# A half pair's value matmuls in one slot, the 64x64 group first: a thresholded attention with a routed MLP

## The chip, the cores and the metric

The kernel runs on one core of a Trainium2 chip. The metric is the device time of one execution in microseconds. The kernel before took 994.81 us (median of three runs, 994.56 to 995.75).

A core has engines that each work through a queue of their own in order: TensorE (PE; its weight loads are listed as PEld), VectorE (DVE), ScalarE (ACT), GpSimd (POOL) and SyncE (SP, which issues most of the transfers). They wait for each other by semaphores. TensorE writes to PSUM, from where VectorE and ScalarE read; everything else lies in SBUF.

## The reference, cut to what matters

```
q, k, v: (8 batches, 8 heads, 576 positions, 64), tau = 0.02
scores = q @ k^T / sqrt(64)
thresh = max(scores, last axis) - tau
scores = where(scores >= thresh, scores, -1e9)
attn   = exp(scores - max);  attn = attn / (sum(attn) + 1e-9)
x      = (attn @ v), as 4608 rows of 512

logits = x @ w_gate                                   # 8 experts, 576 rows each
take the (row, expert) pairs by falling logit, skip rows that have an expert
and experts that are full
out[rows of e] = relu(x[rows of e] @ w1[e]) @ w2[e]   # 512 -> 1024 -> 512
```

The change lies in the first part, the attention, and there in the product attn @ v.

## The kernel before, in words

**Pairs, tiles, slots.** The 64 heads are worked on as 32 pairs p (batch b = p // 4, j = p % 4). A pair has nine score tiles of 128 rows and 576 columns: tile i < 8 holds 128 queries of head i % 2, and tile 8, the short tile, holds the last 64 queries of both heads. The 288 tiles run through a pipeline of slots with two tiles each. In slot s the tiles 2s+4 and 2s+5 get their scores, 2s+2 and 2s+3 are masked, 2s and 2s+1 are transposed. Nine slots are two pairs, so a slot's place is told by its number modulo 9, its *class*; slots 0 to 8 are classes 0 to 8. The short tile of an even pair is scored in class 2 (first of the two tiles), that of an odd pair in class 6 (second).

**What a tile goes through.** `score` (L60) makes the scores with TensorE, in a PSUM tile `sc` of two banks; there are two such tiles. An ordinary tile is two matmuls on 64 rows and 128 columns of the array (64*128 in the profile), a short tile four on 64x64. `mx` (L71) scales them on VectorE into `z` and takes the row minimum of the negated scores (L74), which frees `sc`; GpSimd adds tau (L75). `ex` takes the exponential on ScalarE (L86). A slot later `stt` masks the result on VectorE and sums it (L90). Then `tr` transposes the tile with TensorE (L98, 64*128 as well) into the one PSUM tile `tb`, and in the next slot `trev` copies it on ScalarE into `pt` (L113, L115). Columns 512 to 575 of all tiles are transposed apart: `left` (L117) puts them into unused columns of the second `sc` tile of the slot, and `leftev` (L122) copies them on ScalarE into `pl` (L125 to L128). This is done in classes 4 and 8 (first part) and 5 and 0 (second part).

**Values.** attn @ v of a pair is made in two halves f of the queries: columns 0 to 255 (f=0) and 256 to 575 (f=1), each in a PSUM bank of its own, both named `xo`. A half has four units (`pv_unit`, L140): each two matmuls with all 128 rows and 64 columns of the array (128*64, L146). Keys that don't fit into these blocks are added by `pl_unit` (L147): two matmuls for each half, four in all on four 64x64 tiles of the array (L154), called the group here. Half 0 needs tiles 0 to 3 of a pair transposed, half 1 and the group need all nine. When a half is complete ScalarE copies it to `xt` (L155).

**Gates.** When the fourth pair of a batch is done, `finish` queues four pieces for the router's logits (`lg_unit` for either half, `lgt_unit`, `lgm_unit`), and in batches 0 and 1 five pieces that turn x back to rows and copy it out (`xt_unit`, L215 on VectorE). Each has TensorE work and, a slot later, ScalarE or VectorE work; they take the second `xo` bank in turn with half 1.

**What sets the order.** Every engine's instructions are in the order in which the Python code issues them. A slot issues: the scores, the left transposes, the copies left over from the slot before (`flush`, L255), `trev`, `mx`, `ex`, `leftev`, `stt`, loads for pair p+2 behind the short tile's scores, then `columns` (L259) and `whole` (L273), and last `tr`. `columns` takes units from the head of a queue that `push_pair` (L226) fills, in the order half 0, half 1, group. It spreads them: the number for a slot is what is left of the pair at the head, divided by the slots up to `last_slot` (L258). That makes one or two units, or one or two units and the group, in every slot. `whole` issues at most one gate a slot, when the second bank is free.

After the last scores (slot 141) the rest is issued without limit: the last two pairs' values, the logits of the last batch, and the preparation of the router for the first seven batches (`R.prep` and `R.compare`, L372 on VectorE). The routed MLP behind it (L787, L819 and others) isn't touched.

Of the kernel before, what the change touches and what calls it, by code (L numbers as in the profile page):

```python
# [13 lines left out]
AF = mybir.ActivationFunctionType  # L14
# [8 lines left out]
def attention(ctx, tc, qk, vl, tau, wgd, xrows, xts, Lg, nb_batches, ident, swap, R, after_first):  # L23
    nc=tc.nc
    V=nc.vector; A=nc.scalar; G=nc.gpsimd; T=nc.tensor
    NP=nb_batches*4; NT=NP*9
# [10 lines left out]
    LD={}  # L37
# [22 lines left out]
    def score(t):  # L60

        p,i=divmod(t,9); kd=LD[p]
        sc=ps_s.tile([128,2,512],F32,name="sc"); SC[t]=sc
        if i<8: todo=((i%2,slice(0,128),slice(i//2*128,i//2*128+128)),)
        else: todo=((0,slice(0,64),slice(512,576)),(1,slice(64,128),slice(512,576)))
        for h,o,c in todo:
            for f in range(2):
                r=slice(64*f,64*f+64)
                T.matmul(sc[o,f,:HS], kd["q",h][r,c], kd["k",h][r,:],start=True,stop=True)  # L69
# [25 lines left out]
    PT={}; PL={}; TB={}  # L95
# [36 lines left out]
    have={}  # L132
    XT={}; XO={}

    banks=([[True]],[[True]])
    def bank_v(sh,n):
        banks[n].append([False])
        return ps_v.tile(sh,F32,name="xo%d"%n)
    def free_v(n): return banks[n][-1][0]
    def pv_unit(p,f,u):  # L140
        b,j=divmod(p,4)
        if b not in XT: XT[b]=wk.tile([128,4,S],F32,name="xt",bufs=XTB)
        if u==0: XO[p,f]=bank_v([128,512],f)
        xo=XO[p,f]; q=FQ[f]; v=LD[p]["v"]
        for h in range(2):
            T.matmul(xo[64*h:64*h+64,:q.stop-q.start],v[:,f,128*u+64*h:128*u+64*h+64],PT[p][:,h,u,q],start=(u==0),stop=False,skip_group_check=True)  # L146
    def pl_unit(p,fs=(0,1)):  # L147

        b,j=divmod(p,4); r=[]
        for f in fs:  # L150
            xo=XO.pop((p,f)); q=FQ[f]; n=q.stop-q.start
            for a in range(2):
                g=slice(64*a,64*a+64); h=a^f
                T.matmul(xo[64*h:64*h+64,:n],LD[p]["v"][g,f,512:576],PL[p][g,q],start=False,stop=True,skip_group_check=True)  # L154
            r.append((banks[f][-1],lambda xo=xo,q=q,n=n: A.activation(XT[b][:,j,q],xo[:,:n],AF.Copy)))  # L155
        have[p,"pv"]=1
        return r
    def bank_g(b,sh):
        if b<nb_batches-1: return bank_v(sh,1)
        t=ps_s.tile([128,2,512],F32,name="sc")[:,0]  # L160
        return t.rearrange("p (a b) -> p a b",a=sh[1]) if len(sh)==3 else t

    RD={}
    def rd_calc(b):
        rd=wk.tile([128,4,9],F32,name="rd",bufs=XTB+NBO); RD[b]=rd
        V.tensor_scalar(rd,DEN[b],1e-9,None,op0=ALU.add)
        V.reciprocal(rd,rd)
    LT={}
    def lg_unit(b,f):
        if f==0: LT[b]=wk.tile([128,S+D],F32,name="lt",bufs=LTB)  # L170
        ps=bank_g(b,[128,512]); q=FQ[f]; n=q.stop-q.start; rd=RD[b]
        for j in range(4):
            T.matmul(ps[32*j:32*j+32,:n],wg[:,j],XT[b][:,j,q],start=True,stop=True,tile_position=(0,32*j))  # L173
# [51 lines left out]
    queue=[]; aux=[]; later=[]; late=[]; late2=[]; st={"last":-9,"slot":0}  # L225
    def push_pair(p):  # L226
        b,j=divmod(p,4)
        def when(n): return lambda: have.get((p,n),1<<30)+HOLD<=st["slot"]
        if p==NP-1:


            def left(f):
                for k,g in pl_unit(p,(f,)): g(); k[0]=True
            for f in range(2):
                for u in range(4): queue.append(("c",when("t3" if f==0 else "t8"),0 if u else f+1,lambda f=f,u=u: pv_unit(p,f,u),p))
                if f==0: queue.append(("n",when("t8"),False,lambda: rd_calc(b),p))
            for g in (lambda: left(0),lambda: left(1),lambda: lg_unit(b,0)(),lambda: lg_unit(b,1)(),lambda: lgt_unit(b)(),lambda: lgm_unit(b)()):
                queue.append(("n",when("pl"),False,g,p))
            queue.append(("n",lambda: not later,False,lambda: late.extend([lambda k,c=c: xt_unit(b,c,k) for c in range(5)]),p))
            return  # L240
        for f in range(2):
            for u in range(4): queue.append(("c",when("t3" if f==0 else "t8"),0 if u else f+1,lambda f=f,u=u: pv_unit(p,f,u),p))
            if (f,j)==(0,3): queue.append(("n",when("t8"),False,lambda: rd_calc(b),p))
        queue.append(("c",when("pl"),False,lambda: pl_unit(p),p))
        if (b,j)==(0,0): queue.append(("n",lambda: True,False,R.consts,p))
        if (b,j)==(nb_batches-1,2): queue.append(("n",lambda: not aux,False,lambda: (R.prep(0,28),R.compare(R.k("E1"),J,0,28)),p))
        if j==3: queue.append(("n",lambda: not later,False,lambda: finish(b),p))
    def finish(b):
        aux.extend([(0,lambda: lg_unit(b,0)),(0,lambda: lg_unit(b,1)),(1,lambda: lgt_unit(b)),(0,lambda: lgm_unit(b))])
        rows=[lambda k=1,c=c: xt_unit(b,c,k) for c in range(5)]  # L250
        if nb_batches-NDEF-NBO<=b<nb_batches-NDEF:
            nc.sync.dma_start(xts[b],XT[b]); late2.extend(rows)
        elif b<nb_batches-NDEF: aux.extend([(0,x) for x in rows])
        else: late.extend(rows)
# [32 lines left out]
    for s_ in range(-2,NT//2+2):  # L287
        st["slot"]=s_
        sc_=[t for t in (2*s_+4,2*s_+5) if 0<=t<NT]; tr_=[t for t in (2*s_,2*s_+1) if 0<=t<NT]
        ev_=[t for t in (2*s_-2,2*s_-1) if 0<=t<NT]; tt_=[t for t in (2*s_+2,2*s_+3) if 0<=t<NT]  # L290
        p8=[(t//9,n) for n,x in enumerate((tr_,ev_)) for t in x if t%9==8]
        for t in sc_: score(t)
        for p,n in p8: left(p,n,sc_[-1] if sc_ else None)

        flush()
        for t in ev_:
            p,i=divmod(t,9)
            while i==0 and p>1 and (p-2,"pv") not in have: columns(True); flush()
            trev(t); have[p,f"t{i}"]=s_
        if ev_ and ev_[-1]==NT-1: columns(True)  # L300
        for t in ev_:
            p,i=divmod(t,9)
            if i==3: push_pair(p)
            if i==8: have[p,"pl"]=s_
        for t in sc_: mx(t)
        for t in sc_[:1]: ex(t)
        for p,n in p8: leftev(p,n)
        for t in sc_[1:]: ex(t)
        for t in tt_: stt(t)
        for t in sc_:  # L310
# [4 lines left out]
        if not sc_: columns(True); whole()  # L315
    st["slot"]+=9
    while queue or aux or later:
        st["slot"]+=1; flush(); columns(True); whole()
# [638 lines left out]
```

## Time and profile before

| | |
|---|---|
| median of three runs | 994.81 us |
| profiled execution | 1003.83 us, span 1001.9 us, mean granted clock 0.983 |
| attention, first mx (5.51 us) to that of slot 141 (453.47 us) | 447.96 us for 143 slots |
| first value unit of the last pair | 462.03 us |
| DVE, mx (L74), 288 of them | 205.7 us, mean 750 ns |
| DVE, stt (L90), 256 with `pp` | 199.8 us, mean 812 ns |
| PE, scores (L69) / units (L146) | 181.2 us / 155.7 us |

A row of the timeline gives start, length, engine, line, operation, the names out<-in, the tile of the array for PE, the shape and the number of merged instructions; in brackets stands how long the engine was idle ahead of it and what ended that. An fp32 matmul shows as two records, so a unit is x4 and the group x8. On VectorE the next instruction starts before the record of the last one ends, so the distance of two starts is the better price. A row of the waits gives who waited for what, the total, the number of times and the longest.

### The profile page before, as it was taken

How to read it: one execution, taken by the hardware profiler on the slowest of the kernel's cores; microseconds unless marked ns; L12 is line 12 of the kernel's file. 1: busy time of each engine (PE TensorE's matmuls, PEld its weight loads, DVE VectorE, ACT ScalarE, POOL GpSimd, SP SyncE). 2: the span in 40 equal slices, each digit the busy share in tenths (PEclk: the TensorE clock that was granted, in tenths of full speed). 3: DMA queues.
4: the chain of work that ended last, by engine and by line, in shares of the span. 5: the costliest groups of instructions: out<-in, count | busy, mean ns of one | idle time of the engine just before them, and what ended most of it. 6: DMA issues, size and time to landing. Idle time of an engine off the chain costs nothing.

```text
span 1001.9 us, 24115 instructions
## 1 busy us (share of the span) xinstructions
PE 964.3 (96%) x9141; PEld 710.4 (71%) x9141; DVE 781.2 (78%) x2158; ACT 633.0 (63%) x1257; POOL 261.9 (26%) x411
## 2 busy tenths in 40 slices
PE   7999999999999999998789999999999899999996
PEld 4555655655565555565679798897988879898895
DVE  7999999999999999995669778687787587525220
ACT  6899888888899898986545354253442344545340
POOL 2333443444233333330020213221303003220202
PEclk9999999999999999999979999999999899999998
DMA  6332251451533333203750605242434325241101
GB/s 250 97 119 84 83 182 58 177 184 61 176 111 120 99 117 106 97 3 141 260 199 20 224 30 183 84 152 93 153 106 135 120 70 172 100 156 56 40 11 42
DMA packets 35858, 116.98 MB, mean 117 GB/s; under 512 B 4384, under 2 KB 5024, under 8 KB 35232
## 3 DMA queue, kind: packets, MB, share of 16 engines
q1 hardware_dynamic: 28352, 92.85, 27.1%
q0 software_dynamic: 5888, 19.03, 6.0%
q10 hardware_dynamic: 1504, 3.59, 1.2%
q8 instruction: 72, 1.18, 0.5%
q14 instruction: 42, 0.34, 0.1%
HBM read 93.01 MB, written 21.38 MB: 114 GB/s over the span
## 4 chain that ended last, share of the span: by engine, by line
PE 84%; DVE 8%; issue 3%; DMA 2%; ACT 1%; another core or an unknown queue 0%; POOLq 0%; SPq 0%; DVEq 0%; ACTq 0%
PE pf L787 21%; PE pf L819 19%; PE sc L69 13%; PE xo L146 13%; PE tb L98 8%; DVE pp L90 2%; PE xo L154 2%; PE pt L732 2%; DVE z L74 2%; PE xo L207 1%; PE rps L440 1%; PE xo L173 1%; DMA out_dram<-y,idx 1%; PE sc L98 1%; DVE cmp L372 1%
## 5 line engine op out<-in xcount | busy, mean ns | idle before, releaser
L75 POOL TENSOR_SCALAR nb<-nb,taub 128x1 f32<-128x1 f32 x288 | 152.6, 530 | 286.2 <-DVE z L74 235.5
L86 ACT ACTIVATE pp<-z,nb 128x576 f32<-128x576 f32 x256 | 193.3, 774 | 39.6 <-DVE z L74 39.1
L74 DVE TENSOR_SCALAR_CACHE_REDUCE z<-sc 128x576 f32<-128x576 f32 x288 | 205.7, 750 | 14.6 <-PE sc L69 13.8
L90 DVE SCALAR_TENSOR_TENSOR pp<-z,nb,pp 128x576 f32<-128x576 f32 x256 | 199.8, 812 | 0.3
L819 PE MATMUL pf<-w2h,H 128*128 128x512 f32 x576 | 195.2, 402 | 0.7 <-DVE H L372 0.7
L69 PE MATMUL sc<-qk 64*128 64x288 f32 (+1 forms) x1280 | 181.2, 427 | 3.4 <-DVE z L74 1.5
L146 PE MATMUL xo<-pt,vt 128*64 128x320 f32 (+1 forms) x1024 | 155.7, 420 | 0.4 <-DVE xr L215 0.3
L113 ACT ACTIVATE pt<-tb 128x512 f32<-128x512 f32 x256 | 139.2, 589 | 3.3 <-PE tb L98 1.7
L819 PE MATMUL pf<-w2l,H 128*128 128x512 f32 x320 | 128.3, 401 | 0.0
L826 POOL DMA_INDIRECT out_dram<-y,idx x40 | 42.8, 1069 | 317.7 <-ACT y L822 244.2
L819 PEld LDWEIGHTS pf<-w2h,H 128*128 128x128 f32 x576 | 106.5, 189 | 21.5 <-DVE H L372 1.6
L69 PEld LDWEIGHTS sc<-qk 64*128 64x128 f32 (+1 forms) x1280 | 93.8, 179 | 33.7 <-DVE z L74 5.7
L98 PEld LDWEIGHTS tb<-ident,pp 64*128 64x128 f32 x2048 | 75.4, 139 | 58.0 <-ACT pp L86 20.1
L787 PE MATMUL pf<-xh,w1h 128*128 128x288 f32 (+2 forms) x512 | 112.0, 306 | 0.7 <-ACT xh L733 0.7
L787 PE MATMUL pf<-xl,w1h 128*128 128x288 f32 (+2 forms) x512 | 111.7, 304 | 0.0
L787 PE MATMUL pf<-xh,w1l 128*128 128x288 f32 (+2 forms) x512 | 111.7, 304 | 0.0
L822 ACT ACTIVATE y<-pf 128x512 f32<-128x512 f32 x40 | 23.9, 597 | 128.8 <-PE pf L819 125.3
L146 PEld LDWEIGHTS xo<-pt,vt 128*64 128x64 f32 x1024 | 60.7, 136 | 57.7 <-issue 27.4
L98 PE MATMUL tb<-ident,pp 64*128 64x64 f32 x2048 | 94.1, 229 | 5.0 <-ACT pt L113 4.8
L799 ACT ACTIVATE hf<-pf 128x576 f32<-128x576 f32 x56 | 36.5, 651 | 96.0 <-PE pf L787 83.0
L787 PEld LDWEIGHTS pf<-xh,w1h 128*128 128x128 f32 x512 | 83.9, 194 | 1.5 <-ACT xh L733 1.1
L787 PEld LDWEIGHTS pf<-xh,w1l 128*128 128x128 f32 x512 | 83.6, 193 | 0.2
(199 smaller groups left out, 1315.5 us busy)
## 6 DMA issues: line engine op xcount, KB each, us to landing
qk<-qk_dram SPq DMA_DIRECT2D x31, 864.0 KB, 4.7
vt<-vl_dram SPq DMA_DIRECT2D x32, 576.0 KB, 5.1
w2s<-w_dram SPq DMA_DIRECT2D x32, 512.0 KB, 5.5
w1s<-w_dram SPq DMA_DIRECT2D x28, 512.0 KB, 5.7
xrows<-pp SPq DMA_DIRECT2D x24, 260.0 KB, 2.8
xts<-xt SPq DMA_DIRECT2D x2, 1152.0 KB
pt<-xts SPq DMA_DIRECT2D x2, 1152.0 KB, 8.1
xrows<-xr SPq DMA_DIRECT2D x8, 260.0 KB, 2.0
```

The source lines that it names most:

```text
L69: T.matmul(sc[o,f,:HS], kd["q",h][r,c], kd["k",h][r,:],start=True,stop=True)
L74: V.tensor_scalar(z,SC.pop(t)[:,:,:HS],-0.125,None,op0=ALU.mult,op1=ALU.min,accum_out=nb[:,0:1])
L75: G.tensor_scalar(nb[:,1:2],nb[:,0:1],taub[:,0:1],None,op0=ALU.add)
L86: A.activation(pview(t),ZB[t].rearrange("p a b -> p (a b)"),AF.Exp,bias=NBI[t][:,0:1],scale=-1.0)
L90: V.scalar_tensor_tensor(pv,ZB.pop(t).rearrange("p a b -> p (a b)"),NBI[t][:,1:2],pv,op0=ALU.is_le,op1=ALU.mult,accum_out=den_of(p)[:,p%4, ...
L98: g=slice(64*r,64*r+64); T.transpose(o[:,r],x[r%len(x)][g],ident[g,g])
L113: A.activation(PT[p][:,i%2,:,(i//2)*128:(i//2+1)*128].rearrange("p k (r q) -> p r k q",r=2),tb,AF.Copy)
L146: T.matmul(xo[64*h:64*h+64,:q.stop-q.start],v[:,f,128*u+64*h:128*u+64*h+64],PT[p][:,h,u,q],start=(u==0),stop=False,skip_group_check=True)
L787: T.matmul(ps[:,h,:n],s[w][:,k,f*128:(f+1)*128],s[x][:,k,cols[h]],start=(i==0),stop=(i==11))
L799: A.activation(hf,ps[:,:,:HS],AF.Relu)
L819: T.matmul(ps[:,0,:],H[:,f,c:c+128],s[w][:,f],start=(f==0 and j==0),stop=e)
L826: G.indirect_dma_start(out=out,out_offset=IOA(ap=s["idx"][:n,t:t+1],axis=0),in_=y[:n],in_offset=None)
```

## The change

The units of a half are issued all in one slot: half 0 of an even pair in class 4 and of an odd pair in class 8, the group and half 1 of an even pair in class 6 and of an odd pair in class 2 (nine slots on: 9*(p//2)+11). The group comes ahead of the units of half 1: it ends half 0, which is then copied out, and opens half 1. Both of these slots score a short tile, and in class 2 the two scores change places, so that the short tile is last and the group stands right behind it. The queue's entries carry the slot from which they may be issued; `last_slot` and the spreading are gone, and `columns` no longer stops behind a finished half. `whole` issues a gate only in a slot in which `columns` issued no unit, except while more than four gates wait. The last pair keeps its order.

```
-    def pv_unit(p,f,u):
+    def evict(p,f):
+        b,j=divmod(p,4); xo=XO.pop((p,f)); q=FQ[f]
+        return banks[f][-1],lambda: A.activation(XT[b][:,j,q],xo[:,:q.stop-q.start],AF.Copy)
+    def pv_unit(p,f,u,first=True,last=False):
...
-        if u==0: XO[p,f]=bank_v([128,512],f)
+        if (p,f) not in XO: XO[p,f]=bank_v([128,512],f)
...
-            T.matmul(xo[64*h:64*h+64,:q.stop-q.start],v[:,f,128*u+64*h:128*u+64*h+64],PT[p][:,h,u,q],start=(u==0),stop=False,skip_group_check=True)
-    def pl_unit(p,fs=(0,1)):
+            T.matmul(xo[64*h:64*h+64,:q.stop-q.start],v[:,f,128*u+64*h:128*u+64*h+64],PT[p][:,h,u,q],start=first and u==0,stop=last and u==3,skip_group_check=True)
+        if last and u==3:
+            have[p,"pv"]=1
+            return [evict(p,f)]
+    def pl_unit(p,fs=(0,1),first=()):
...
+        return [evict(p,f) for f in fs if f not in first]
...
-        for f in range(2):
-            for u in range(4): queue.append(("c",when("t3" if f==0 else "t8"),0 if u else f+1,lambda f=f,u=u: pv_unit(p,f,u),p))
-            if (f,j)==(0,3): queue.append(("n",when("t8"),False,lambda: rd_calc(b),p))
-        queue.append(("c",when("pl"),False,lambda: pl_unit(p),p))
+        a=9*(p//2)+(8 if p%2 else 4); e=9*(p//2)+(11 if p%2 else 6)
+        for u in range(4): queue.append(("c",when("t3"),0 if u else 1,lambda u=u: pv_unit(p,0,u),a))
+        if j==3: queue.append(("n",when("t8"),0,lambda: rd_calc(b),p))
+        queue.append(("c",when("pl"),2,lambda: pl_unit(p,first=(1,)),e))
+        for u in range(4): queue.append(("c",when("t8"),0,lambda u=u: pv_unit(p,1,u,False,True),e))
...
-    def last_slot(p): return 9*(p//2)+(12 if p%2 else 8 if p<NP-2 else 7)
     def columns(all=False):
-        c=[x[4] for x in queue if x[0]=="c"]
-        if not c: n=9
-        else: n=9 if all else max(1,c.count(c[0])//max(1,last_slot(c[0])-st["slot"]+1))
+        n=0
         while queue and queue[0][1]():
-            k,_,first,g,p=queue[0]
+            k,_,first,g,at=queue[0]
             if k=="c":
-                if n==0: return
-                if first and not free_v(first-1): return
-                n-=1
+                if not all and st["slot"]<at: return n
+                if first and not free_v(first-1): return n
+                n+=1
             queue.pop(0); r=g()
-            if k=="c" and r:
-                later.extend(r)
-                return
-    def whole():
-        if aux and free_v(1) and st["slot"]>=st["last"]+aux[0][0]:
+            if k=="c" and r: later.extend(r)
+        return n
+    def whole(n):
+        if aux and free_v(1) and st["slot"]>=st["last"]+aux[0][0] and (n==0 or len(aux)>4):
...
+        if sc_ and sc_[0]%9==8: sc_.reverse()
         for t in sc_: score(t)
...
-        if sc_: columns(); whole()
+        if sc_: whole(columns())
         for t in tr_: tr(t,t==tr_[0])
```

More of the change, by code (lines that the diff above doesn't have):

```diff
@@ L139, in free_v @@
     def free_v(n): return banks[n][-1][0]
-    def pv_unit(p,f,u):
+    def evict(p,f):
+        b,j=divmod(p,4); xo=XO.pop((p,f)); q=FQ[f]
+        return banks[f][-1],lambda: A.activation(XT[b][:,j,q],xo[:,:q.stop-q.start],AF.Copy)
+    def pv_unit(p,f,u,first=True,last=False):
         b,j=divmod(p,4)
         if b not in XT: XT[b]=wk.tile([128,4,S],F32,name="xt",bufs=XTB)
-        if u==0: XO[p,f]=bank_v([128,512],f)
+        if (p,f) not in XO: XO[p,f]=bank_v([128,512],f)
         xo=XO[p,f]; q=FQ[f]; v=LD[p]["v"]
         for h in range(2):
-            T.matmul(xo[64*h:64*h+64,:q.stop-q.start],v[:,f,128*u+64*h:128*u+64*h+64],PT[p][:,h,u,q],start=(u==0),stop=False,skip_group_check=True)
-    def pl_unit(p,fs=(0,1)):
-        b,j=divmod(p,4); r=[]
+            T.matmul(xo[64*h:64*h+64,:q.stop-q.start],v[:,f,128*u+64*h:128*u+64*h+64],PT[p][:,h,u,q],start=first and u==0,stop=last and u==3,skip_group_check=True)
[3 more added lines that the diff above has]
+    def pl_unit(p,fs=(0,1),first=()):
         for f in fs:
-            xo=XO.pop((p,f)); q=FQ[f]; n=q.stop-q.start
+            if (p,f) not in XO: XO[p,f]=bank_v([128,512],f)
+            xo=XO[p,f]; q=FQ[f]
             for a in range(2):
                 g=slice(64*a,64*a+64); h=a^f
[L154 to L157, printed above, removed]
+                T.matmul(xo[64*h:64*h+64,:q.stop-q.start],LD[p]["v"][g,f,512:576],PL[p][g,q],start=f in first,stop=f not in first,skip_group_check=True)
+        return [evict(p,f) for f in fs if f not in first]
     def bank_g(b,sh):
@@ L229, in push_pair @@
         if p==NP-1:
+            a=9*(p//2)+8
             def left(f):
@@ L234, in push_pair @@
             for f in range(2):
-                for u in range(4): queue.append(("c",when("t3" if f==0 else "t8"),0 if u else f+1,lambda f=f,u=u: pv_unit(p,f,u),p))
+                for u in range(4): queue.append(("c",when("t3" if f==0 else "t8"),0 if u else f+1,lambda f=f,u=u: pv_unit(p,f,u),a))
                 if f==0: queue.append(("n",when("t8"),False,lambda: rd_calc(b),p))
@@ L240, in push_pair @@
             return
-        for f in range(2):
-            for u in range(4): queue.append(("c",when("t3" if f==0 else "t8"),0 if u else f+1,lambda f=f,u=u: pv_unit(p,f,u),p))
-            if (f,j)==(0,3): queue.append(("n",when("t8"),False,lambda: rd_calc(b),p))
-        queue.append(("c",when("pl"),False,lambda: pl_unit(p),p))
+        a=9*(p//2)+(8 if p%2 else 4); e=9*(p//2)+(11 if p%2 else 6)
[3 more added lines that the diff above has]
+        for u in range(4): queue.append(("c",when("t8"),0,lambda u=u: pv_unit(p,1,u,False,True),e))
         if (b,j)==(0,0): queue.append(("n",lambda: True,False,R.consts,p))
@@ L312, in attention @@
             if i==8 and p+2<NP: load(p+2)
-        if sc_: columns(); whole()
+        if sc_: whole(columns())
         for t in tr_: tr(t,t==tr_[0])
-        if not sc_: columns(True); whole()
+        if not sc_: whole(columns(True) and 0)
     st["slot"]+=9
     while queue or aux or later:
-        st["slot"]+=1; flush(); columns(True); whole()
+        st["slot"]+=1; flush(); whole(columns(True) and 0)
     for k in range(0,NBO,2):
```

## The prediction

> **What bounds the kernel now.** I read the page first, then the busy time by stretches, then the waits of VectorE, and last the timeline of some slots. The change touches the attention stage alone, which lasts to about 466 us. Its beat is the slot: two score tiles, so two mx (L74) and two stt (L90) on VectorE. The stretches below start and end where the first mx of slots -2, 18, 54 and 141 starts; the fourth is one batch, slots 90 to 107. Columns: length, then busy time of PE, PEld, DVE, ACT, POOL, clock, DMA.
>
> ```profile
> PE 964.3 (96%) x9141; PEld 710.4 (71%) x9141; DVE 781.2 (78%) x2158; ACT 633.0 (63%) x1257; POOL 261.9 (26%) x411
> ```
>
> ```profile
> 5.51:64.76 59.25, 53.41 (x622) 31.40 (x622) 57.93 (x174) 49.84 (x93) 20.73 (x43) 0.97 0.45 162
> 64.76:180.19 115.43, 115.37 (x1370) 68.02 (x1368) 111.99 (x315) 101.37 (x197) 42.32 (x80) 1.00 0.32 109
> 180.19:453.47 273.28, 272.53 (x3267) 159.85 (x3267) 265.09 (x756) 245.33 (x478) 98.44 (x183) 1.00 0.33 111
> 294.71:350.46 55.75, 55.75 (x673) 32.65 (x671) 54.17 (x155) 50.54 (x99) 19.38 (x37) 1.00 0.33 108
> ```
>
> ```profile
> DVE z L74 <- PE sc L69: 9.1, 25, 0.7
> ```
>
> PE shows 100% there, but the end of a matmul is modelled, so that is no proof. VectorE is the surer clock: it idles 59.25 - 57.93 = 1.32, 115.43 - 111.99 = 3.44 and 273.28 - 265.09 = 8.19 us, 12.95 us in all, and in the steady part (from 50 to 454 us) 9.1 us of it is mx waiting for scores. **No order of PE's work can win more than these 12.95 us before the tail**, as VectorE's own work stays. What an order can lose has no such limit.
>
> How the two engines hold each other is read from single slots. First class 2 to 4 (slot number modulo 9) as they are:
>
> ```profile
> 356.64 0.69 DVE L74 TENSOR_SCALAR_CACHE_REDUCE z<-sc 128x576 f32<-128x576 f32 x1
> 358.54 1.19 PE L69 MATMUL sc<-qk 64*128 64x288 f32 x8
> 359.42 0.75 DVE L74 TENSOR_SCALAR_CACHE_REDUCE z<-sc 128x576 f32<-128x576 f32 x1
> 359.66 1.30 PE L146 MATMUL xo<-pt,vt 128*64 128x320 f32 x8
> 360.89 0.77 PE L154 MATMUL xo<-pl,vt 64*64 64x256 f32 x8
> 361.59 0.71 PE L98 MATMUL tb<-ident,pp 64*128 64x64 f32 x16
> 362.13 1.19 PE L69 MATMUL sc<-qk 64*128 64x288 f32 x8
> 362.89 0.76 DVE L74 TENSOR_SCALAR_CACHE_REDUCE z<-sc 128x576 f32<-128x576 f32 x1 [0.55 <-PE sc L69]
> 363.43 0.65 PE L146 MATMUL xo<-pt,vt 128*64 128x256 f32 x4
> ```
>
> From start to start PE spends 1.12 us on two scores with the change of tile shape behind them, 1.23 on two value units of the 320-column half, 0.70 on the group of four, 0.54 on the transposes; mx starts 0.76 after the scores (362.13 to 362.89). That slot is too long for VectorE, which waits 0.55. With the first left transposes between scores and values it is 1.30 (362.13 to 363.43).
>
> **How far PE can run ahead.** There are two score tiles in PSUM. The first score of a slot needs its tile back from the first mx of the slot before. The start of the stage shows slots without value units, just what the change makes of classes 0, 1, 3, 5 and 7:
>
> ```profile
> 8.14 0.76 DVE L74 TENSOR_SCALAR_CACHE_REDUCE z<-sc 128x576 f32<-128x576 f32 x1 [1.18 <-PE sc L69]
> 8.96 1.70 PE L69 MATMUL sc<-qk 64*128 64x288 f32 x6 [0.37 <-DVE z L74]
> 13.82 0.75 DVE L74 TENSOR_SCALAR_CACHE_REDUCE z<-sc 128x576 f32<-128x576 f32 x1
> 14.25 0.71 PE L98 MATMUL tb<-ident,pp 64*128 64x64 f32 x16 [0.87 <-ACT pt L113]
> 14.90 1.40 PE L69 MATMUL sc<-qk 64*64 64x288 f32 x12
> 16.65 0.75 DVE L74 TENSOR_SCALAR_CACHE_REDUCE z<-sc 128x576 f32<-128x576 f32 x1
> 25.16 0.75 DVE L74 TENSOR_SCALAR_CACHE_REDUCE z<-sc 128x576 f32<-128x576 f32 x1
> 26.52 0.70 PE L69 MATMUL sc<-qk 64*128 64x288 f32 x4
> 27.42 0.71 PE L69 MATMUL sc<-qk 64*64 64x288 f32 x8 [0.19 <-ACT pl L128]
> ```
>
> VectorE left alone needs 16.65 - 13.82 = 2.83, about 2.84 us a slot. The next slot's score starts 0.82 us after an mx start at best (8.14 to 8.96). In light slots it starts 14.90 - 13.82 = 1.08 after it, since the transposes ahead of it in PE's queue wait for ScalarE to empty their only bank (the 0.87). Into class 6 it starts 26.52 - 25.16 = 1.36 after it, and the second score waits 0.19 more, as ScalarE reads the left transposes out of that tile. So **a light slot doesn't bank its spare time**: PE waits, at most one slot ahead.
>
> **The change part by part.** The prices of PE's pieces stand in these rows, from slots 140 and 141 and from the tail, where four units already run in one go:
>
> ```profile
> 451.11 1.08 PE L146 MATMUL xo<-pt,vt 128*64 128x256 f32 x8
> 452.13 0.71 PE L98 MATMUL tb<-ident,pp 64*128 64x64 f32 x16
> 452.68 1.35 PE L69 MATMUL sc<-qk 64*128 64x288 f32 x12
> 453.96 1.30 PE L146 MATMUL xo<-pt,vt 128*64 128x320 f32 x8
> 462.03 1.95 PE L146 MATMUL xo<-pt,vt 128*64 128x256 f32 x16
> 463.91 0.28 PE L98 MATMUL sc<-ident,pp 64*128 64x64 f32 x2
> 464.18 2.37 PE L146 MATMUL xo<-pt,vt 128*64 128x320 f32 x16
> 466.48 0.77 PE L154 MATMUL xo<-pl,vt 64*64 64x256 f32 x8
> ```
>
> Two units of 256 columns take 1.02 (451.11 to 452.13), four take 1.88 (462.03 to 463.91): two more cost 0.86, so one change of shape costs about 1.02 - 0.86 = 0.16. For 320 columns 1.23 and 2.30 (464.18 to 466.48) give 0.16 as well. Transposes cost 0.55 (452.13 to 452.68).
>
> *Removed:* changes of shape. Scores and transposes have one shape (64*128), value units another, group and short tile a third. Counted through the code, nine slots have 23 changes now and 10 after: 13 x 0.16 = 2.1 us less PE work per two pairs. The Trainium skill, "TensorEngine Tiling (Array Packing)", Key Properties, says that a change of tiling mode drains TensorE. The trace agrees in kind, with 0.16 us here; by this rule alone the kernel gets faster, which is the third rival.
>
> *Moved, classes 2 and 6:* the scores with the short tile second cost 1.28 up to the values (452.68 to 453.96). The group comes in between: 0.70 less its own change, 0.54 if the shape of the short tile carries over, 0.70 if it doesn't; I take 0.54, as both rows name 64*64. Then 2.30 and 0.55. From score start to score start 1.28 + 0.54 + 2.30 + 0.55 = 4.67, and to the next mx 4.67 + 0.76 = 5.43. Behind an mx start in the slot before, that mx comes 1.08 + 5.43 = 6.51 us later in class 2 and 1.36 + 0.19 + 5.43 = 6.98 in class 6. VectorE alone would need 2 x 2.84 = 5.68. **So VectorE waits 0.83 and 1.30 us** at these joins; at the best lead, 0.82 + 5.43 - 5.68 = 0.57. Queued behind on PE are the transposes, and behind those ScalarE's read-out.
>
> *Moved, classes 4 and 8:* 1.30 + 1.88 + 0.55 + 0.76 = 4.49, with the lead of 1.08 it is 5.57, under 5.68. Nothing is lost, but the cover is 0.11 us: what makes these slots longer shows in full.
>
> *Nothing:* the copies of the group's result are the same two, behind the same flush, and ScalarE has 55.75 - 50.54 = 5.2 us free per batch. Loads keep their slots (behind the short tile's scores) and find their buffers free no later; SP carries little else there. The group needs the read-out that freed the score tile at 27.42, so it adds no wait. The 320-column bank, which the gates share, is read out after a gate of class 1 or 5 at the start of the next slot, before the group comes; POOL's small copies go with the gates. Turning the scores of class 2 round saves one of the changes counted above.
>
> *Gates:* they go into light slots, which have room. While more than four wait (batches 0 and 1, with the xr copies) some share a full slot, and there they count:
>
> ```profile
> 367.70 0.75 PE L173 MATMUL xo<-xt,wg 128*32 128x320 f32 x8
> 368.38 0.71 PE L98 MATMUL tb<-ident,pp 64*128 64x64 f32 x16
> ```
>
> Such a gate takes 0.68, less the 0.11 it is 0.57, once in class 4 of either batch; the copies that fall into class 8 follow gates that give VectorE work of its own.
>
> The sum, in idle time of VectorE. Before a wait the last instruction's read of the accumulator counts as busy:
>
> ```profile
> L74 DVE DVE_READ_ACCUMULATOR z<-sc 128x1 f32 x72 | 5.9, 81 | 0.0
> ```
>
> So a join shows as 0.75 or 1.22. To slot 18: 1.18 from the start (the row at 8.14), the join of slot 6 is hidden by the constants made on VectorE behind it, then 0.75 + 1.22: 3.15 against 1.32. Slots 18 to 53: eight joins, 7.9; VectorE's copies stand beside about half of them (bounds 0 and 7.9), so I take half, 3.9, and 2 x 0.49 for the gates: 4.9 against 3.44. Slots 54 to 140: ten of class 2, nine of class 6: 7.5 + 11.0 = 18.5 against 8.19. Together 26.5 against 12.95: **+13.6 us**.
>
> *The tail.* Preparing the router now follows pair 30's last unit in slot 141 instead of slot 143, so ahead of the last two stt:
>
> ```profile
> 453.47 0.75 DVE L74 TENSOR_SCALAR_CACHE_REDUCE z<-sc 128x576 f32<-128x576 f32 x1
> 457.79 0.38 DVE L372 TENSOR_REDUCE b<-Lg 128x28 f32<-128x224 f32 x1
> 460.67 0.17 DVE L166 TENSOR_SCALAR rd<-den 128x36 f32<-128x36 f32 x1
> ```
>
> It takes 460.67 - 457.79 = 2.88. The last transposes start some 453.47 -> 457.79 = 4.32, plus 2.88 and 0.1, so 7.3 us after that mx, the last pair's units 0.55 behind, at some 7.9; they start at 462.03 - 453.47 = 8.56 now, with units and group of pair 30 ahead of them. I take -0.6; if the join of slot 141 is added here it is +0.7.
>
> So +13.0. The profiled execution took 1003.83 us (span 1001.9, 1.9 around it), 9.0 over the median 994.81; it would take 1016.8. Nothing shows the attention stage to be what differs, so I carry the 13.0 over: **1007.8 us**. A difference under 0.2% (2 us) can't be told from none.
>
> **The rivals.** *Longer full slots still:* the group's shape doesn't carry over, or its four matmuls go one after the other, so 4.67 grows by 0.16 to 0.6; or classes 4 and 8 lose their 0.11. At 0.3 us more in each full slot, 29 joins give 8.7 and 31 slots of classes 4 and 8 give 31 x 0.19 = 5.9, so +14.6: about 1022. For: those slots never stood in this order. Against: the short tile's four ran together, 0.70 is the price of four.
>
> *No difference:* PE enters every join with the lead of 0.82: a join shows as 0.49, so 1.18 + 1.0 to slot 18, 2.0 + 1.0 to slot 54 and 19 x 0.49 = 9.3 behind it, 14.5 against 12.95; with the tail +0.9, 996. For: the gates' VectorE work in light slots lets PE catch up. Against: the 1.08 and 1.36 of the start.
>
> *Faster:* PE's total sets the beat, and 2.1 us less per nine slots is more than VectorE's idle time there (1.58 per 18, from the fourth stretch). It decides if a full slot costs less than 5.68 - 1.36 - 0.19 - 0.76 = 3.37 instead of 4.67 us. Then the 12.95 go, less the 1.18: 994.8 - 11.8 - 0.6, about 982. For: PE's 100%. Against: two score tiles, and the start's waits, where PE stands 0.87 us behind ScalarE and 0.37 behind an mx. The Trainium skill, "Perfetto Trace Analysis", Optimization Strategy, says that the same gap coming back can mean too few buffers for the next tile; those two rows agree, and by that page the joins stay.
>
> **How the numbers follow.** Joins hold VectorE: 0.66, and by itself 1003 to 1014, from the copies' bounds (3.9 either way) and the tail's. Longer still: 0.14. No difference: 0.11, a hundredth of it counted as faster. Faster: 0.09. The range 995 to 1018 leaves out the faster case and the worse half of the longer one. Faster by over 0.2%: 0.10; within: 0.10; slower: 0.66 + 0.14 = 0.80.
>
> **What would show it.** Right: VectorE waits for scores at the first mx of classes 3 and 7 alone, 0.7 to 1.3 us each, some 26 times, and the attention stage grows by about 13 us; four units and group at 2.3 and 0.54; no wait in classes 5 and 0; light slots with PE waiting for ScalarE. Wrong: waits under 0.5 at those places, or waits at classes 5 and 0, or a difference that lies behind 470 us.

## The result, and the profile after

The kernel after takes 1019.12 us (median of four runs, 1017.13 to 1021.05), the kernel before 994.68 us (four runs, 994.3 to 995.75). The ratio is 1.0244, with a 95% interval of 1.0221 to 1.0267: 24.4 us slower, where 13.0 were predicted.

The busy time by stretches of the kernel after, cut as in the prediction at the first mx (L74) of slots -2, 18, 54 and 141; the second to last row is the same stage in one piece, and the last one is everything from the group of the last pair on. Columns: length, then PE, PEld, DVE, ACT, POOL, clock, DMA.

```profile
5.47:67.55 62.08, 54.83 (x640) 33.43 (x640) 58.12 (x173) 51.42 (x94) 20.97 (x43) 1.00 0.44 162
67.55:192.69 125.14, 118.09 (x1386) 72.76 (x1384) 114.26 (x321) 102.99 (x197) 47.16 (x84) 1.00 0.33 115
192.69:477.31 284.62, 265.59 (x3245) 163.11 (x3245) 261.60 (x754) 247.24 (x476) 92.14 (x179) 1.00 0.29 98
5.47:477.31 471.84, 438.51 (x5263) 269.30 (x5265) 433.98 (x1246) 401.65 (x765) 160.27 (x306) 1.00 0.32 111
489.47:1016.30 526.83, 505.57 (x3748) 439.59 (x3746) 338.60 (x884) 228.08 (x476) 99.41 (x97) 0.98 0.36 117
```

The same two views of the kernel before:

```profile
5.51:453.47 447.96, 441.31 (x5255) 259.27 (x5257) 435.01 (x1244) 396.54 (x765) 161.49 (x306) 1.00 0.34 117
466.48:1001.90 535.42, 509.02 (x3748) 442.63 (x3746) 337.62 (x884) 227.91 (x476) 98.79 (x97) 0.97 0.35 115
```

The attention stage grows from 447.96 to 471.84 us, **by 23.9 us**, and that is the whole loss. VectorE's busy time hardly moves (435.01 to 433.98); its idle time goes from 12.95 to 471.84 - 433.98 = 37.86 us. PE, which in the prediction's rows of before had almost no idle time from slot 18 on (0.06 and 0.75 us), now has 125.14 - 118.09 = 7.1 and 284.62 - 265.59 = 19.0 us in the second and third stretch. So both engines stand still more, at different times. VectorE waits for scores behind the long slots; PE waits in the light ones, for ScalarE to empty the only bank of the transposes, 24.8 us in all where it was 2.7 before, and 18 us of it in classes 0 and 1:

```profile
PE tb L98 <- ACT pt L113: 19.2, 37, 1.0
PE tb L98 <- ACT pt L115: 5.6, 13, 0.5
```

The two profiled executions differ by less, 1018.22 - 1003.83 = 14.4 us. The last row of each view shows why: behind the attention the one of before took 535.42 and that of after 526.83 us for the same work. That would account for most of the 9 us by which the profiled execution of before lies above its median; so the stages are what can be compared, not the spans. What made it slower there isn't explained.

VectorE's waits for scores over the stage, first in the kernel after, then in the kernel before (total, number of times, longest):

```profile
DVE z L74 <- PE sc L69: 39.5, 35, 3.5
```

```profile
DVE z L74 <- PE sc L69: 13.8, 27, 3.5
```

The waits grow by 25.7 us, a little more than the stage. They sit almost all where the prediction put them: at the first mx behind the two heavy slots (classes 2 and 6). Class 2 waits 0.82 to 0.85 us in ten of fifteen slots, class 6 1.29 or 1.30 in five of fourteen. Most of the others are of two kinds, 1.79 (five) and 1.52 (four), and these two carry most of what the prediction lacked.

An ordinary join, from slot 105 (class 6) into slot 106 (class 7), in the timeline of after:

```profile
356.65 0.75 DVE L74 TENSOR_SCALAR_CACHE_REDUCE z<-sc 128x576 f32<-128x576 f32 x1
358.08 1.55 PE L69 MATMUL sc<-qk 64*128 64x288 f32 x12
359.45 0.71 PE L160 MATMUL xo<-pl,vt 64*64 64x256 f32 x8
360.10 2.37 PE L149 MATMUL xo<-pt,vt 128*64 128x320 f32 x16
362.40 0.71 PE L98 MATMUL tb<-ident,pp 64*128 64x64 f32 x16
362.95 1.19 PE L69 MATMUL sc<-qk 64*128 64x288 f32 x8
363.70 0.76 DVE L74 TENSOR_SCALAR_CACHE_REDUCE z<-sc 128x576 f32<-128x576 f32 x1 [1.30 <-PE sc L69]
```

PE starts the scores 358.08 - 356.65 = 1.43 us behind the mx of the slot before; scores and group up to the values take 2.02 (about 0.2 of waiting for ScalarE inside the scores included), the four units 2.30, the transposes 0.55, and the mx comes 363.70 - 356.65 = 7.05 us after the earlier one, where VectorE alone would need about 5.68. Every piece is the predicted one (the sum there was 6.98).

A join behind a logits gate in class 5, slot 96:

```profile
327.10 0.75 PE L177 MATMUL xo<-xt,wg 128*32 128x320 f32 x8
328.61 0.45 ACT L128 ACTIVATE pl<-sc 64x64 f32<-64x64 f32 x2
328.96 0.76 ACT L86 ACTIVATE pp<-z,nb 128x576 f32<-128x576 f32 x1
329.63 0.42 ACT L182 ACTIVATE lt<-xo 128x320 f32<-128x320 f32 x1
329.65 1.21 PE L160 MATMUL xo<-pl,vt 64*64 64x256 f32 x8
330.79 2.37 PE L149 MATMUL xo<-pt,vt 128*64 128x320 f32 x16
334.39 0.76 DVE L74 TENSOR_SCALAR_CACHE_REDUCE z<-sc 128x576 f32<-128x576 f32 x1 [1.79 <-PE sc L69]
```

Here the group lasts from 329.65 to 330.79, 1.14 us instead of 359.45 to 360.10, 0.65. Its second half opens the bank that the gate has used, and ScalarE's copy of that gate (L182), though it is issued ahead of the group, starts at 329.63 only, behind a left read-out (L128) and an exponential in ScalarE's queue. The 0.49 us reappear in full in the join: 1.79 for 1.30. This happens in slots 60, 78, 96, 114 and 132.

A join behind one of batch 0's copies, slot 29, class 2:

```profile
103.53 1.35 PE L69 MATMUL sc<-qk 64*128 64x288 f32 x12
104.69 0.61 PE L160 MATMUL xo<-pl,vt 64*64 64x256 f32 x4
105.09 0.68 DVE L219 COPY xr<-xo 128x512 f32<-128x512 f32 x1
105.69 0.74 DVE L74 TENSOR_SCALAR_CACHE_REDUCE z<-sc 128x576 f32<-128x576 f32 x1
105.82 0.76 PE L160 MATMUL xo<-pl,vt 64*64 64x320 f32 x4 [0.52 <-DVE xr L219]
106.51 2.37 PE L149 MATMUL xo<-pt,vt 128*64 128x320 f32 x16
110.12 0.76 DVE L74 TENSOR_SCALAR_CACHE_REDUCE z<-sc 128x576 f32<-128x576 f32 x1 [1.52 <-PE sc L69]
```

The reader of the bank is now VectorE itself (L219). PE can open the bank at 105.82, 0.13 behind the start of the mx that follows the copy, and from there 0.69 of group, 2.30 of values, 0.55 and 0.76 lead to the next first mx: 4.43 us, whatever lead PE had. Four joins (slots 29, 33, 47, 51) show this 1.52.

Behind slot 141 the tail is 485.02 - 477.31 = 7.71 us up to the last pair's values, where it was 8.56:

```profile
477.31 0.75 DVE L74 TENSOR_SCALAR_CACHE_REDUCE z<-sc 128x576 f32<-128x576 f32 x1
485.02 1.95 PE L149 MATMUL xo<-pt,vt 128*64 128x256 f32 x16
```

### The profile page after: what moved, and what is told of

The parts are those of the page before. It is cut to its first block, busy times and chain, and to the rows that moved or that the text cites. A ratio compares the mean times of both kernels' runs of the same rounds, so it can differ in the third digit from the quotient of the medians.

```text
span 1016.3 us, 24038 instructions
## 1 busy us (share of the span) xinstructions
PE 957.3 (94%) x9141; PEld 717.3 (71%) x9141; DVE 781.3 (77%) x2158; ACT 638.4 (63%) x1257; POOL 261.3 (26%) x411
## 3 DMA queue, kind: packets, MB, share of 16 engines
q8 instruction: 72, 1.18, 0.5%
## 4 chain that ended last, share of the span: by engine, by line
PE 63%; DVE 14%; ACT 11%; issue 8%; DMA 2%; DVEq 0%; POOLq 0%; SPq 0%; ACTq 0%
PE pf L789 21%; PE pf L821 19%; PE xo L149 8%; ACT pp L86 5%; PE sc L69 5%; DVE z L74 4%; DVE pp L90 4%; PE tb L98 3%; ACT pt L113 2%; PE xo L160 2%; PE pt L734 2%; DVE pm L90 2%; ACT pl L128 1%; PE rps L442 1%; ACT pl L125 1%
## 5 line engine op out<-in xcount | busy, mean ns | idle before, releaser
L74 DVE TENSOR_SCALAR_CACHE_REDUCE z<-sc 128x576 f32<-128x576 f32 x288 | 205.5, 749 | 39.8 <-PE sc L69 39.5
L69 PE MATMUL sc<-qk 64*128 64x288 f32 (+1 forms) x1280 | 186.6, 430 | 5.4 <-ACT pl L128 0.9
L149 PE MATMUL xo<-pt,vt 128*64 128x320 f32 (+1 forms) x1024 | 138.3, 412 | 0.0
L98 PEld LDWEIGHTS tb<-ident,pp 64*128 64x128 f32 x2048 | 75.1, 138 | 70.8 <-ACT pt L113 39.5
L821 PEld LDWEIGHTS pf<-w2h,H 128*128 128x128 f32 x576 | 106.5, 189 | 19.9 <-DVE H L374 1.5
L149 PEld LDWEIGHTS xo<-pt,vt 128*64 128x64 f32 x1024 | 67.8, 136 | 55.3 <-issue 15.1
L824 ACT ACTIVATE y<-pf 128x512 f32<-128x512 f32 x40 | 23.9, 598 | 127.0 <-PE pf L821 123.6
```

The source lines that it names most:

```text
L74: V.tensor_scalar(z,SC.pop(t)[:,:,:HS],-0.125,None,op0=ALU.mult,op1=ALU.min,accum_out=nb[:,0:1])
L98: g=slice(64*r,64*r+64); T.transpose(o[:,r],x[r%len(x)][g],ident[g,g])
L821: T.matmul(ps[:,0,:],H[:,f,c:c+128],s[w][:,f],start=(f==0 and j==0),stop=e)
```

## The experiments

Theory A, as the expectations call it: a join costs what the slot's lump of PE work exceeds two slots of VectorE by, since PE is never more than one slot ahead; behind some joins the wait for the shared bank comes on top. What stands against it is told in each expectation. Runs of one group share their runs of the kernel before: 998.7 us (median of 13) for the first four, 1000.03 us (median of 17) for the last three. Times are therefore compared as ratios, and the stage by its length in the profile, from the first mx to that of slot 141.

| kernel | us | ratio to before, 95% | stage, us | waits for scores, us |
|---|---|---|---|---|
| before | | 1 | 447.96 | 13.8 |
| after | 1019.12 | 1.0244 (1.0221 to 1.0267) | 471.84 | 39.5 |
| gates away from classes 1 and 5 | 1018.13 | 1.0185 (1.0143 to 1.0226) | 467.84 | 35.3 |
| two units a slot | 998.96 | 0.9996 (0.9974 to 1.0019) | 449.49 | 15.9 |
| group last | 1025.20 | 1.0249 (1.0209 to 1.0289) | 474.08 | 42.3 |
| whole pair in one slot | 1076.86 | 1.0764 (1.0699 to 1.0829) | 523.31 | 90.5 |
| even pair's group in a slot of its own | 995.80 | 0.9960 (0.9938 to 0.9982) | 442.17 | 10.0 |
| first half spread | 1022.15 | 1.0222 (1.0193 to 1.0252) | 471.20 | 39.1 |
| second half spread | 1017.96 | 1.0170 (1.0141 to 1.0199) | 468.67 | 31.8 |

**Gates away from classes 1 and 5.** No gate right ahead of a slot with the group.

```
-        if aux and free_v(1) and st["slot"]>=st["last"]+aux[0][0] and (n==0 or len(aux)>4):
+        if aux and free_v(1) and st["slot"]>=st["last"]+aux[0][0] and (n==0 or len(aux)>4) and st["slot"]%9 not in (1,5):
```

> The changed kernel, with no gate in classes 1 and 5, the slots ahead of the joins. Theory A (two causes: the full slot is too long for VectorE, and the group's opening of the shared bank waits for the read-out of a gate issued one slot ahead): the five class 6 joins behind a logits gate fall from 1.79 to 1.30 us of waiting, the four joins behind a copy gate from 1.52 to 0.85 to 1.3; about 4 us in all, 1015 us. Theory B (only the length of the slot counts, the bank costs nothing): the joins stay as they are, 1019 us.

The stage shrinks by 4.0 us to 467.84. A class 6 join in its timeline:

```profile
207.73 0.71 PE L160 MATMUL xo<-pl,vt 64*64 64x256 f32 x8
208.37 2.38 PE L149 MATMUL xo<-pt,vt 128*64 128x320 f32 x16
211.98 0.76 DVE L74 TENSOR_SCALAR_CACHE_REDUCE z<-sc 128x576 f32<-128x576 f32 x1 [1.30 <-PE sc L69]
```

The group is back at 208.37 - 207.73 = 0.64 us, no class 6 join shows more than 1.30, and the joins of 1.52 fall to 0.68 and 0.48 in class 2 and to 1.30 in class 6. The moved gates change other joins too: they cost 0.31 at four slots of class 0, make one class 2 join of 1.59 and bring two class 6 joins from 0.96 to 1.30 and 1.18; two of class 2 fall from 0.82 to 0.23 and 0.22, where a copy on VectorE (L219) now stands in class 0. So the shared bank holds PE behind those gates, and moving them is worth 4 us of the loss in all; the other 19.9 us of the stage are there without it. The ratios alone can't show it, as their intervals touch.

**Two units a slot.** The order of after (group first, its place, the swapped scores), but the units of each half spread over two slots, and the gates in classes 0, 4 and 8, beside two units.

```
-        for u in range(4): queue.append(("c",when("t3"),0 if u else 1,lambda u=u: pv_unit(p,0,u),a))
+        for u in range(4): queue.append(("c",when("t3"),0 if u else 1,lambda u=u: pv_unit(p,0,u),a+u//2))
...
-        for u in range(4): queue.append(("c",when("t8"),0,lambda u=u: pv_unit(p,1,u,False,True),e))
+        for u in range(4): queue.append(("c",when("t8"),0,lambda u=u: pv_unit(p,1,u,False,True),e+u//2))
...
-        if aux and free_v(1) and st["slot"]>=st["last"]+aux[0][0] and (n==0 or len(aux)>4):
+        if aux and free_v(1) and st["slot"]>=st["last"]+aux[0][0] and (st["slot"]%9 in (0,4,8) or len(aux)>4):
```

> The changed kernel with the units of a half pair in two neighbouring slots, two each (classes 4 and 5, 6 and 7, 8 and 0, 2 and 3); the group stays right behind the short tile's scores, the scores of class 2 stay turned round, gates go into classes 0, 4 and 8. Theory A (a full slot is too long): the class 6 slot falls from 4.67 to 4.67 - 1.07 = 3.60 us of TensorE, no join waits over 0.3 us, and the time is that of before within some 4 us: 991 to 998. Theory C (the group's new place, the turned scores or the order of the queue cost the time, not the four units): it stays above 1010 us.

```profile
5.52:455.01 449.49, 436.05 (x5263) 264.31 (x5265) 434.71 (x1244) 400.33 (x765) 158.45 (x306) 1.00 0.34 117
```

22.35 of the 23.9 us are gone. The waits that are left show 0.19 to 0.66 us each, more than the expected 0.3, and the time can't be told from that of before. Nothing but the spreading and the gates' places differs from after, and the gates alone gave 4: **the four units in one slot are the cause** of most of the loss.

**Group last.** In the same slot the four units come first and open the bank; the group follows and ends both halves.

```
+        if not first: have[p,"pv"]=1
...
-        queue.append(("c",when("pl"),2,lambda: pl_unit(p,first=(1,)),e))
-        for u in range(4): queue.append(("c",when("t8"),0,lambda u=u: pv_unit(p,1,u,False,True),e))
+        for u in range(4): queue.append(("c",when("t8"),0 if u else 2,lambda u=u: pv_unit(p,1,u),e))
+        queue.append(("c",when("pl"),0,lambda: pl_unit(p),e))
```

> The changed kernel with the group behind the four units of the second half, in the same slot. Everything else stays. Theory A: the group pays its own change of shape again, 0.16 us in each of 31 joins, on the path: 5 us more, 1024 us. If the shape of the short tile did not carry over to the group anyway: 1019 us.

```profile
361.19 2.37 PE L149 MATMUL xo<-pt,vt 128*64 128x320 f32 x16
363.49 0.77 PE L160 MATMUL xo<-pl,vt 64*64 64x256 f32 x8
364.19 0.71 PE L98 MATMUL tb<-ident,pp 64*128 64x64 f32 x16
365.50 0.76 DVE L74 TENSOR_SCALAR_CACHE_REDUCE z<-sc 128x576 f32<-128x576 f32 x1 [1.47 <-PE sc L69]
```

Ordinary joins grow by one change of shape: 1.30 to 1.47, and 0.82 to 0.99 in class 2. So the shape of the short tile's scores does carry over to the group in the order of after, and a change costs 0.16 to 0.17 us. Where the bank is awaited the joins stay (1.53, 0.97, 1.80): there the opening of the bank decides, not what stands ahead of it. The stage grows by 2.24 us only, less than the 5 expected, for that reason.

**Whole pair in one slot.** Half 0 too goes into the slot of half 1, eight units and the group.

```
-        for u in range(4): queue.append(("c",when("t3"),0 if u else 1,lambda u=u: pv_unit(p,0,u),a))
+        for u in range(4): queue.append(("c",when("t3"),0 if u else 1,lambda u=u: pv_unit(p,0,u),e))
```

> The changed kernel with the first half's four units in the same slot as the group and the second half, ahead of the group: eight units and the group in classes 2 and 6, nothing in 4 and 8. Theory A (VectorE can be fed only one slot ahead, so TensorE's time in a single slot counts): each of 29 joins waits 1.71 + 0.32 = 2.0 us longer, 58 us more, 1077 us. Rival (TensorE's work over a period counts): two more changes of shape per join, 0.32 x 31 = 10 us, 1029 us.

```profile
394.87 1.54 PE L69 MATMUL sc<-qk 64*128 64x288 f32 x12
396.35 1.95 PE L149 MATMUL xo<-pt,vt 128*64 128x256 f32 x16
398.23 0.77 PE L160 MATMUL xo<-pl,vt 64*64 64x256 f32 x8
398.92 2.37 PE L149 MATMUL xo<-pt,vt 128*64 128x320 f32 x16
402.53 0.76 DVE L74 TENSOR_SCALAR_CACHE_REDUCE z<-sc 128x576 f32<-128x576 f32 x1 [3.34 <-PE sc L69]
```

The total of PE's work is the same (the trace counts 236 changes of shape in the stage, against 234 in after), yet the stage grows by another 51.5 us in its profile; there were two runs. Most joins with nothing beside them grow by 2.0 (0.82 to 2.81, 1.30 to 3.34): the 1.88 of four more units and a change of shape. Five of class 2 grow by 2.2 to 2.8. Those that still stand behind a gate show 2.39 to 2.41 only, where after had 1.79, 1.52 or 0.96: VectorE's own work on the gate (1.18 us for L194 and L195 in class 5, 0.68 for L219 in class 1) covers part of the wait, and the first units run before PE needs the bank. So 51.5 came where 58 were expected; how much of the difference is the one and how much the other wasn't parted.

**Only the first half spread, only the second half spread.**

```
-        for u in range(4): queue.append(("c",when("t3"),0 if u else 1,lambda u=u: pv_unit(p,0,u),a))
+        for u in range(4): queue.append(("c",when("t3"),0 if u else 1,lambda u=u: pv_unit(p,0,u),a+u//2))
```

> The changed kernel with only the first half's units spread, two in classes 4 and 5 and two in 8 and 0; group and four units of the second half stay in one slot. Theory A: the joins in classes 2 and 6 set the cost, and four units of the first half behind a light slot cost nothing, so nothing is won: an attention stage of 470 to 474 us, some 1019 us for the kernel (2.2 to 2.6% over before). Rival (each full slot costs its share): about half the loss is gone, 1.2% over before.

The stage is 471.20 us, 0.6 shorter than after, with 39.1 us of waits: the lump of half 0 (classes 4 and 8) costs nothing by itself, as the prediction had it. The rule for gates sends them to other slots here, so the 1.79 are gone, while class 2 shows 0.96 in five slots behind gates that came into class 1, and 1.52 in four slots instead of two.

```
-        for u in range(4): queue.append(("c",when("t8"),0,lambda u=u: pv_unit(p,1,u,False,True),e))
+        for u in range(4): queue.append(("c",when("t8"),0,lambda u=u: pv_unit(p,1,u,False,True),e+u//2))
...
-        if aux and free_v(1) and st["slot"]>=st["last"]+aux[0][0] and (n==0 or len(aux)>4):
+        if aux and free_v(1) and st["slot"]>=st["last"]+aux[0][0] and (st["slot"]%9 in (0,1,5) or len(aux)>4):
```

> The changed kernel with only the second half's units spread, group and two units in classes 2 and 6, two more in 3 and 7; the first half's four units stay in one slot (classes 4 and 8); gates in 0, 1 and 5. Theory A (a long slot is free only behind a light one): the joins fall to some 0.3 to 0.6 us, but classes 4 and 8 now follow slots with two units, TensorE has no lead there, and about 0.9 us of waiting shows up in classes 5 and 0; an attention stage of 465 to 473 us. Rival (only the joins are too long): the waits of the joins fall and nothing takes their place, the time is within 0.5% of before.

The timeline of a class 7 slot with two units (slot 115) and a class 8 slot with four, up to the first mx of class 0:

```profile
389.95 0.76 DVE L74 TENSOR_SCALAR_CACHE_REDUCE z<-sc 128x576 f32<-128x576 f32 x1 [0.29 <-PE sc L69]
392.09 1.19 PE L69 MATMUL sc<-qk 64*128 64x288 f32 x8
393.39 1.95 PE L149 MATMUL xo<-pt,vt 128*64 128x256 f32 x16
395.81 1.19 PE L69 MATMUL sc<-qk 64*128 64x288 f32 x8
396.57 0.76 DVE L74 TENSOR_SCALAR_CACHE_REDUCE z<-sc 128x576 f32<-128x576 f32 x1 [0.80 <-PE sc L69]
```

The joins behind the second half fall to 0.19 to 0.59, but 28 waits, most of them 0.70 or 0.80 us, appear at the first mx of classes 5 and 0, where after had 0.36 twice. The slot of half 0 hasn't changed; the slot ahead of it has. PE starts its scores 392.09 - 389.95 = 2.14 us behind the mx, where after mostly shows 1.14 to 1.50, so the 4.49 us of that slot no longer fit. A long slot is free only behind a light one, which is why neither half alone brings back what both do.

**An even pair's group in a slot of its own.** Two units in a slot, and none in class 6 beside the group: half 1 of an even pair starts a slot later, half 0 of an odd pair moves to class 0. Class 2 keeps the group and two units. Gates go to classes 0, 4 and 5.

```
-        a=9*(p//2)+(8 if p%2 else 4); e=9*(p//2)+(11 if p%2 else 6)
-        for u in range(4): queue.append(("c",when("t3"),0 if u else 1,lambda u=u: pv_unit(p,0,u),a))
+        a=9*(p//2)+(9 if p%2 else 4); e=9*(p//2)+(11 if p%2 else 6)
+        for u in range(4): queue.append(("c",when("t3"),0 if u else 1,lambda u=u: pv_unit(p,0,u),a+u//2))
...
-        for u in range(4): queue.append(("c",when("t8"),0,lambda u=u: pv_unit(p,1,u,False,True),e))
+        for u in range(4): queue.append(("c",when("t8"),0,lambda u=u: pv_unit(p,1,u,False,True),e+u//2+1-p%2))
...
-        if aux and free_v(1) and st["slot"]>=st["last"]+aux[0][0] and (n==0 or len(aux)>4):
+        if aux and free_v(1) and st["slot"]>=st["last"]+aux[0][0] and (st["slot"]%9 in (0,4,5) or len(aux)>4):
```

> Units two a slot with every place worked out forward from the rows measured so far: first half in classes 4 and 5 (even pair) and 0 and 1 (odd pair), the group in class 6 by itself with the second half's units in 7 and 8, and in class 2 with two units and two more in class 3; gates in 0, 4 and 5. The group stays right behind the short tile's scores. Theory A (a slot may be long only if the slot ahead of it is short, and the shared bank must not be awaited): waits for scores fall under those of before, 13.8 us, the attention stage gets about 7 us shorter than before, and the kernel is 0.7% faster than before (0.990 to 0.997). Rival (the spread over nine slots is worth nothing beyond the two-a-slot kernel): within 0.2% of before.

Its stretch, and a class 6 slot with the group and no unit:

```profile
5.47:447.64 442.17, 434.27 (x5257) 263.67 (x5259) 433.30 (x1244) 396.77 (x765) 162.01 (x306) 1.00 0.34 119
```

```profile
336.92 1.35 PE L69 MATMUL sc<-qk 64*128 64x288 f32 x12
338.08 0.71 PE L160 MATMUL xo<-pl,vt 64*64 64x256 f32 x8
339.45 1.19 PE L69 MATMUL sc<-qk 64*128 64x288 f32 x8
340.69 0.74 DVE L74 TENSOR_SCALAR_CACHE_REDUCE z<-sc 128x576 f32<-128x576 f32 x1
```

The slot takes 339.45 - 336.92 = 2.53 us from score to score, under VectorE's 2.84, and the mx at 340.69 waits for nothing. No wait stands at the first mx of class 7 in the whole stage. The stage is 5.8 us shorter than before (7 were expected) and the time 0.4% shorter (0.2 to 0.6%; 0.7% was expected): this kernel beats after clearly and before by a little.

## Why the prediction was right or wrong, point by point

**Bound and direction: right.** VectorE's beat and the joins behind classes 2 and 6 set the stage; classes 4 and 8 cost nothing; the light slots don't bank their time. The whole loss lies in the attention stage, and two units a slot takes it back. The Trainium skill, "Perfetto Trace Analysis", Optimization Strategy, which says that a gap that comes back can mean too few buffers, fits these joins; no run here had a third score tile, so the number of tiles itself wasn't tried.

**Prices of the pieces: right; the lead into class 2: wrong, and hidden by luck.** Group 0.65 with the change behind it, four units 2.30 and 1.88, transposes 0.55, change of shape 0.16 to 0.17, the group's shape carried over. In the last stretch class 2's ten joins add to 7.61 us (7.5 predicted). That agreement is luck: slot 11, which has no other work on VectorE beside it, waits 1.27. Its rows show a lead of 43.73 - 42.13 = 1.60 us, where the prediction took 1.08 from the first slots:

```profile
42.13 0.75 DVE L74 TENSOR_SCALAR_CACHE_REDUCE z<-sc 128x576 f32<-128x576 f32 x1
43.73 1.35 PE L69 MATMUL sc<-qk 64*128 64x288 f32 x12
48.39 0.95 PE L69 MATMUL sc<-qk 64*128 64x288 f32 x6
```

The slot itself takes 48.39 - 43.73 = 4.66, against 4.67 in the sum. Seven later slots that show 0.82 or 0.83 have the lead of 1.60 as well; there VectorE's own 0.55 us in class 1 (L170, L171) makes up for most of the 0.52 by which the lead was too small. Where VectorE's own work falls into class 0 (L204, L205), the lead is 1.17 or 0.94, and the joins show 0.85 and 0.47. This was read from the trace and not tested.

**The step that failed first: the bank that the gates share.** The prediction put it under nothing, because the bank "is read out after a gate of class 1 or 5 at the start of the next slot, before the group comes". It is *issued* before; it is *done* later, as ScalarE has a left read-out and exponentials ahead of it. In the last stretch this makes 5 x 0.49 = 2.45 us: class 6's nine joins add to 14.14 where 11.0 were predicted, the rest being 0.08 a join.

**The step that failed most: "VectorE's copies stand beside about half of them (bounds 0 and 7.9), so I take half, 3.9".** The eight joins of slots 18 to 53 show 9.65 us, above even the upper bound of 7.9. None of them was hidden, which alone is the half that was left out. A copy was taken as VectorE work that covers the wait; but the copy holds the very bank that PE needs next (the 0.52 in the row at 105.82), so PE's slot starts late and the four joins behind copies show 1.52, more than the 0.75 and 1.22 of a join without any. With gates and copies moved to other slots the same joins show 0.68 and 0.48 in class 2 and 1.30 in class 6; as VectorE's work has moved there too, that run alone doesn't part the two. Both ends of the bound came from one mechanism (cover), and the other (the bank) wasn't priced.

**The gates in class 4:** 0.36 each, 0.49 predicted; slightly too dear.

**The sum.** In the profile the stage grew by 23.9 us where 13.6 were predicted. Idle time of VectorE was predicted at 3.15, 4.9 and 18.5 us and measured at 62.08 - 58.12 = 3.96, 125.14 - 114.26 = 10.88 and 284.62 - 261.60 = 23.02. Of the 11.3 us missing, 5.7 are the eight joins of the second stretch, 3.1 class 6 in the third, 0.6 the two joins of the first; the rest, some 2, are small gaps beside the joins. The prediction priced joins alone and compared them with all idle time of before, small gaps included.

**The tail:** -0.85, predicted -0.6; right.

**The rivals.** *Longer full slots still* gave 1022, near the measured time, but neither of its mechanisms is what happened: the shape carries over, and classes 5 and 0 show no wait but the two behind gates. *No difference* fell: waits of 0.47 or 0.48, which it wanted at all joins, stand at two joins of class 2. *Faster* fell with its premise. PE's busy time did sink in the stage, from 441.31 to 438.51 us, but its idle time is 471.84 - 438.51 = 33.3 us now: what fewer changes of shape save goes into waiting. The changes did become fewer: with the gates included the trace counts 397 in the stage of before and 234 in that of after, 51 and 29 in the slots 90 to 107. The units' busy time falls with them, from 148.8 to 131.6 us, but that of scores and groups grows by 5.6 and 5.1, in part by waits that show as longer rows, as at 329.65. The Trainium skill, "TensorEngine Tiling (Array Packing)", Key Properties, says that a change of mode drains TensorE; the runs show a price for a change, 0.16 to 0.17 us, not the drain itself, and that price is too small beside what grouping the work costs. The kernel with an even pair's group in a slot of its own shows that a better order could still win 5.8 us of the stage's 12.95 us of idle time.

## What to carry to other kernels

Where two buffers join two engines that work in order, count the work of one engine slot by slot, not over a period: a lump is free only if it fits with the lead that the slot ahead of it leaves, and here the saved changes of shape didn't pay for it. For each bank that two kinds of work share, look when its last reader *ends* in that engine's queue, behind everything that stands there, and price the next opening from that point. Work of the waiting engine counts as cover only if it doesn't hold what the other engine needs.

## What the runs showed of the hardware

A change of the TensorE tile's shape costs 0.16 to 0.17 us in these fp32 matmuls, whether between 128*64 and 64*128 or between 64*64 and 128*64, and a group of 64*64 matmuls behind scores of the same shape pays none: moving the group behind the units made each free join 0.17 longer. The group's second half alone takes 0.69 us (105.82 to 106.51), no less than all four matmuls together (0.65, from 359.45 to 360.10): on four 64*64 tiles the halves run side by side, and a wait for one bank puts them one behind the other. Opening a PSUM bank whose reader is late shows as a longer group on PE (1.14 for 0.65 us), once with a releaser named and once without one: the row at 329.65 has no bracket, so such a wait is found by comparing lengths of the same group, not in the list of waits.
